# Attention scores as three 64-row products interleaved with half transposes, in one periodic order of all engines

## Chip, cores, metric

The kernel runs on 1 core of one Trainium2 chip. The metric is the device time of one execution in microseconds (us). The program is one launch; the changed part is its first stage.

## The reference

```
q_rot, k_rot = rotate(q), rotate(k)                      # rotary embedding, B=4, H=8, S=576, D=64
scores = q_rot @ k_rot.T / 8;  scores -= max
attn = exp(scores);  attn /= sum + 1e-9;  x = attn @ v   # to (2304, 512)
h = x @ w_in;  g = where(h > 0, h, exp(min(h, 0)) - 1);  x = g @ w_out     # 512 -> 2048 -> 512
out = ((x @ w1) * (x @ w2)) @ w3 @ w_out2                # 512 -> 1024 -> 1024 -> 512
```

All inputs are float32; the weights are drawn so that their words are unpacked from 64-bit words on the chip.

## The kernel before

**Stage one, attention, is the part that the change rewrites.** A unit is one batch and one pair of heads; there are 16 units. The two heads of a pair lie on 64 partitions each (D = 64). For every unit the kernel loads q and k (`load`, L267, on SP's queue), rotates them on POOL (`rope`: two multiplications with the cosine and sine table L284, one addition L287), copies the high part to a reduced-precision form on ACT (`copy_hi`, L94) and makes the low part on POOL (L293). A score is hi*hi + hi*lo + lo*hi. So that one product of 128 rows does two of these terms, `stack` (L363) copies the parts by 12 DMAs of 144 KB a unit into a tile `st` in which high and low lie on top of each other.

**Groups.** A unit has nine score groups (c, j): four blocks c of 128 queries for each of the two heads j, and one group c = 4 for the last 64 queries of both heads at once (`scores`: L388 takes 4 products from `st`; c = 4 takes 6 products of L380, from the block-diagonal tile `diag`, which POOL fills by two small copies, L98). Each group then has a maximum on DVE (L400), an exponential on ACT with the row sums (L404), four 128x128 transposes on TensorE (`turn`, L436, with L444 and L448 for the keys beyond 512) and an evacuation from PSUM, on ACT or DVE in turn (L418, L420). `weigh` multiplies by v (L505, one head in each column half of the array; L495, L499). `norm`, `spread` (POOL, L98) and `norm_turn` (L477, L479) make the reciprocal sums, spread and transpose them; `weighed` (L511) multiplies them in.

**Order.** The order of every engine is written out by hand: a loop over groups n issues group n+2's scores and softmax and group n's transposes, and a table `todo` holds what else comes at each n (rotation, loads, sums, weights). Unit 0 runs its scores from 64-row products (L380), since its stacks would come too late; dummy products (`warm_up`, L610) stand between. 16 weight chunks are fetched and unpacked during the stage (`paced`, L136 on ACT; L139, L142, L145 on DVE).

**The rest** (two feed-forward networks, from L739 on) is untouched but for one call. Its first product C at L739 follows the last product of stage one on TensorE.

```
for kc in range(4):                                             # turn
    pe.transpose(pt[:, kc], pr[:, at_:at_ + P], idt)
...
for z in (1, 2):                                                # scores, L388
    pe.matmul(s[:, n, :288], st[:, j, 0, c * P:c * P + P], st[:, j, z, n * 288:(n + 1) * 288], start=(z == 1), stop=(z == 2))
```

Of the kernel before, what the change touches and what calls it, by code (L numbers as in the profile page):

```python
# [7 lines left out]
F32 = mybir.dt.float32  # L8
F32R = mybir.dt.float32r
# [10 lines left out]
NKC = 5  # L20
SK = S + 64
# [28 lines left out]
SUM_STEP = 3  # L50
MAKE_AT = (133, 64, 104)
# [20 lines left out]
def kernel(  # L72
# [161 lines left out]
    with ExitStack() as c1:  # L234
# [17 lines left out]
        ps_t = c1.enter_context(tc.tile_pool(name="ps_t", bufs=3, space=PSUM, reuse_waits="tile"))  # L252

        tab = tab_p.tile([P, 2, 2, SK], F32, name="tab")
        diag = [cst.tile([P, 2, P], F32R, name=f"diag{i}") for i in range(2)]
        two = cst.tile([P, D], F32, name="two")
        pl1 = cst.tile([P, 384], F32, name="plT1")
        zero = cst.tile([P, 1, 1], F32, name="zero")
        sums_b = [cst.tile([P, 6, 2], F32, name=f"sums{i}") for i in range(3)]
        rb = [cst.tile([P, 2, 2, D], F32, name="rb"), cst.tile([P, 3, 2, D], F32, name="rb2")]  # L260

        raws, hls, stacks, vs = {}, {}, {}, {}

        def load(u, w):
            n = (S, SK)[w]
            raws[u, w] = qk_p.tile([P, 2, n], F32, tag="raw_qk", name="raw_qk", padded_shape=[P, 2, SK])
            nc.sync.dma_start(raws[u, w], (q, k)[w][u[0], u[1]])  # L267

        def load_v(u):
            vs[u] = v_p.tile([P, 2 * NKC * D + P], F32, tag="v", name="v_")  # L270
            nc.sync.dma_start(vs[u], v[u[0], u[1]])

        COLS = (slice(0, S), slice(S, S + SK))
        TAB = (slice(SK - S, SK), slice(0, SK))

        def rope(u, w):

            if u not in hls:
                hls[u] = hl_st[units.index(u) % 2].tile([P, 2, 2 * SK], F32R, tag="hl", name="hl")
            hl, r = hls[u], raws[u, w]  # L280
            hi, lo = hl[:, 0, COLS[w]], hl[:, 1, COLS[w]]

            def turn(z):
                pool.tensor_tensor(r[:, z], r[:, z], tab[:, w, z, TAB[w]], op=ALU.mult)  # L284

            def add():
                pool.tensor_tensor(r[:, 0], r[:, 0], r[:, 1], op=ALU.add)  # L287

            def high():
                copy_hi(hi, r[:, 0], act)  # L290

            def low():
                pool.tensor_tensor(lo, r[:, 0], hi.bitcast(F32), op=ALU.subtract)  # L293
                stack(u, w)

                m = units.index(u) + 2 - w
                if m < len(units):
                    load(units[m], 1 - w)

            return [lambda: turn(0), lambda: turn(1), add, high, low]  # L300

        def first_load(u):

            for w in (0, 1):
                raws[u, w] = qk_p.tile([P, 2, (S, SK)[w]], F32, tag="raw_qk", name="raw_qk", padded_shape=[P, 2, SK])
            for dst, src, at_, to in (
                (tab[:, 1], tables, 0, 352), (raws[u, 1], k[u[0], u[1]], 0, 352), (raws[u, 0], q[u[0], u[1]], 0, 256),
                (tab[:, 1], tables, 352, SK), (raws[u, 1], k[u[0], u[1]], 352, SK), (raws[u, 0], q[u[0], u[1]], 256, S),
            ):
                nc.sync.dma_start(dst[:, :, at_:to], src[:, :, at_:to])  # L310

        def part(u, w, at_, to, eng, hi_eng, lo_eng):

            s, c, t = (SCALE, 1.0)[w], COLS[w].start, TAB[w].start

            def turn(z):
                r = raws[u, w]
                eng.tensor_tensor(r[:, z, at_:to], r[:, z, at_:to], tab[:, 1, z, t + at_:t + to], op=ALU.mult)

            def add():  # L320
                r = raws[u, w]
                eng.tensor_tensor(r[:, 0, at_:to], r[:, 0, at_:to], r[:, 1, at_:to], op=ALU.add)

            def high():
                if u not in hls:
                    hls[u] = hl_st[units.index(u) % 2].tile([P, 2, 2 * SK], F32R, tag="hl", name="hl")
                copy_hi(hls[u][:, 0, c + at_:c + to], raws[u, w][:, 0, at_:to], hi_eng, s)

            def low():
                r, hl = raws[u, w][:, 0, at_:to], hls[u][:, :, c + at_:c + to]  # L330
                if s == 1.0:
                    lo_eng.tensor_tensor(hl[:, 1], r, hl[:, 0].bitcast(F32), op=ALU.subtract)
                else:
                    lo_eng.scalar_tensor_tensor(hl[:, 1], r, s, hl[:, 0].bitcast(F32), op0=ALU.mult, op1=ALU.subtract)

            return [lambda: turn(0), lambda: turn(1), add, high, low]

        def first_rope(u):
            for w, at_, to, eng, steps in (
                (1, 0, 352, dve, (0, 1, 2)), (0, 0, 256, dve, (0, 1, 2)),  # L340
                (1, 0, 352, dve, (3, 4)), (0, 0, 256, dve, (3, 4)), (1, 352, SK, dve, (0, 1, 2, 3, 4)),
            ):
                pieces = part(u, w, at_, to, eng, act, eng)
                for k_ in steps:
                    pieces[k_]()
# [20 lines left out]
        HALF = ((0, 256), (256, 320))  # L366
        sums_t, S_t, pr_t, pt_t = {}, {}, {}, {}

        def scores(g):
            u, c, j = g  # L370
            s = S_t[g] = ps_s.tile([P, 2, 512], F32, tag="s", name="s")
            if c == 4 or u == units[0]:

                d, h = diag[units.index(u) % 2], slice(64 * j, 64 * j + 64) if c < 4 else slice(0, P)
                at_ = S + 64 * (c == 4 or j == 0)
                for n in range(2):
                    if n and g == seq[0]:
                        warm_up(FILL_IN)
                    for i, (a, e) in enumerate(PAIRS):
                        pe.matmul(  # L380
                            s[:, n, :288], hls[u][h, a, c * P:c * P + P] if c < 4 else d[:, a],
                            hls[u][h, e, at_ + n * 288:at_ + (n + 1) * 288], start=(i == 0), stop=(i == 2),
                        )
                return
            st = stacks[u]
            for z in (1, 2):
                for n in range(2):
                    pe.matmul(  # L388
                        s[:, n, :288], st[:, j, 0, c * P:c * P + P], st[:, j, z, n * 288:(n + 1) * 288],
                        start=(z == 1), stop=(z == 2),  # L390
                    )
# [1020 lines left out]
```

## Time and profile before

| what | value |
|---|---|
| device time, median of 3 runs | 1001.48 us (997.84 to 1002.62) |
| profiled execution, first to last instruction (span) | 998.8 us |
| stage one (to the first product of L739) | 298.89 us of the span |
| TensorE (PE) busy | 981.7 us, 98% of the span |
| DVE, ACT, POOL busy | 783.3, 643.0, 234.9 us |
| DMA, mean | 161 GB/s |

The profiled execution is known by its span alone; what lies around the span is not in the profile. Busy time of PE counts a product to its modelled end, and products overlap, so a busy share of 98% does not say that PE could not take more. PE is matmuls, PEld its weight loads, SP the engine that issues the loads.

### The profile page before, as it was taken

How to read it: one execution, taken by the hardware profiler on the slowest of the kernel's cores; microseconds unless marked ns; L12 is line 12 of the kernel's file. 1: busy time of each engine (PE TensorE's matmuls, PEld its weight loads, DVE VectorE, ACT ScalarE, POOL GpSimd, SP SyncE). 2: the span in 40 equal slices, each digit the busy share in tenths (PEclk: the TensorE clock that was granted, in tenths of full speed). 3: DMA queues.
4: the chain of work that ended last, by engine and by line, in shares of the span. 5: the costliest groups of instructions: out<-in, count | busy, mean ns of one | idle time of the engine just before them, and what ended most of it. 6: DMA issues, size and time to landing. Idle time of an engine off the chain costs nothing.

```text
span 998.8 us, 16766 instructions
## 1 busy us (share of the span) xinstructions
PE 981.7 (98%) x5900; PEld 863.3 (86%) x5900; DVE 783.3 (78%) x1467; ACT 643.0 (64%) x1373; POOL 234.9 (24%) x242
## 2 busy tenths in 40 slices
PE   9899999999999999999999999999999999999998
PEld 8677777777769999999999999998899999999997
DVE  6588888888869999998889999665657676675544
ACT  3577776776769687897778877774444454444332
POOL 3688889899660000000000000000000000000000
PEclk9899999999999999999999999999999999999999
DMA  5878787887731446676564686514132243224211
GB/s 186 233 234 243 233 251 231 228 255 208 220 120 44 149 152 204 196 213 205 190 194 145 210 280 208 182 61 148 32 121 84 89 140 85 74 74 149 87 30 63
DMA packets 76930, 160.99 MB, mean 161 GB/s; under 512 B 9520, under 2 KB 18352, under 8 KB 76848
## 3 DMA queue, kind: packets, MB, share of 16 engines
q1 hardware_dynamic: 76848, 159.95, 52.7%
q8 instruction: 46, 0.75, 0.3%
q14 instruction: 36, 0.29, 0.1%
HBM read 107.68 MB, written 25.69 MB: 134 GB/s over the span
## 4 chain that ended last, share of the span: by engine, by line
PE 87%; POOL 4%; DMA 4%; DVE 2%; ACT 1%; issue 1%; SPq 0%; ACTq 0%; DVEq 0%; POOLq 0%
PE y L782 13%; PE A L1213 10%; PE A L739 10%; PE o L1239 9%; PE B L739 7%; PE B L1213 7%; PE yb L783 7%; PE o L505 5%; PE w L1143 4%; PE s L388 4%; PE ptp L436 4%; PE s L380 1%; DVE nm L400 1%; DMA st<-hl 1%; PE warm L610 1%
## 5 line engine op out<-in xcount | busy, mean ns | idle before, releaser
L782 PE MATMUL y<-g,wo 128*128 128x512 f32 x576 | 204.1, 392 | 0.0
L783 PE MATMUL yb<-g,wo 128*128 128x256 f32 x576 | 161.2, 280 | 0.0
L404 ACT ACTIVATE pr<-s,nm 128x576 f32<-128x576 f32 x144 | 106.3, 738 | 50.5 <-DVE nm L400 49.9
L153 DVE TENSOR_TENSOR set<-set 128x512 fp32r<-128x512 f32 (+1 forms) x160 | 98.2, 619 | 41.6 <-ACT set L150 41.2
L782 PEld LDWEIGHTS y<-g,wo 128*128 128x128 f32 x576 | 107.8, 187 | 20.5
L400 DVE TENSOR_REDUCE nm<-s 128x1 f32<-128x576 f32 x144 | 108.0, 751 | 17.9 <-PE s L388 9.7
L1213 PE MATMUL A<-xc,set 128*128 128x384 f32 x576 | 116.1, 336 | 0.2
L1239 PE MATMUL o<-W,g 128*128 128x512 f32 x432 | 111.1, 393 | 0.0
L739 PE MATMUL A<-xf,set 128*128 128x384 f32 x552 | 111.1, 336 | 0.0
L1213 PEld LDWEIGHTS A<-xc,set 128*128 128x128 f32 x576 | 102.4, 188 | 7.8 <-DVE p L1300 1.0
L783 PEld LDWEIGHTS yb<-g,wo 128*128 128x128 f32 x576 | 108.7, 189 | 0.0
L388 PE MATMUL s<-st 128*128 128x288 f32 x480 | 94.0, 318 | 4.5 <-DMA st<-hl 3.6
L739 PEld LDWEIGHTS A<-xf,set 128*128 128x128 f32 x552 | 93.7, 188 | 2.9
L94 ACT ACTIVATE g<-p 128x384 fp32r<-128x384 f32 x48 | 25.2, 526 | 107.8 <-DVE p L1300 71.5
L436 PE MATMUL ptp<-idt,pr 128*128 128x128 f32 x576 | 90.8, 280 | 0.6 <-ACT pr L404 0.6
L1239 PEld LDWEIGHTS o<-W,g 128*128 128x128 f32 x432 | 80.0, 188 | 12.7
L150 ACT ACTIVATE set<-set 128x512 fp32r<-128x512 f32 (+1 forms) x160 | 89.1, 568 | 2.6 <-DMA set<-kept 2.4
L436 PEld LDWEIGHTS ptp<-idt,pr 128*128 128x128 f32 x576 | 65.5, 143 | 29.1 <-DVE ri L460 8.0
L1213 PE MATMUL B<-xc,set 128*128 128x384 f32 x432 | 86.5, 334 | 0.0
L284 POOL TENSOR_TENSOR raw_qk<-raw_qk,tab 128x640 f32<-128x640 f32 (+1 forms) x56 | 85.2, 1521 | 2.2
L739 PE MATMUL B<-xf,set 128*128 128x384 f32 x420 | 84.3, 336 | 0.0
L1213 PEld LDWEIGHTS B<-xc,set 128*128 128x128 f32 x432 | 76.0, 188 | 0.0
(378 smaller groups left out, 1834.0 us busy)
## 6 DMA issues: line engine op xcount, KB each, us to landing
set<-kept SPq DMA_DIRECT2D x120, 256.0 KB, 2.8
st<-hl SPq DMA_DIRECT2D x180, 144.0 KB, 2.6
raw<-w_ SPq DMA_DIRECT2D x32, 512.0 KB, 4.2
kept<-wr SPq DMA_DIRECT2D x40, 256.0 KB, 3.2
raw_qk<-k_ SPq DMA_DIRECT2D x15, 640.0 KB, 5.4
raw_qk<-q_ SPq DMA_DIRECT2D x15, 576.0 KB, 4.4
raw<-w_in_ SPq DMA_DIRECT2D x16, 512.0 KB, 5.2
raw<-w_out_ SPq DMA_DIRECT2D x16, 512.0 KB, 5.3
```

The lines of the kernel that those rows point to most:

```text
L150: act.activation(t[:, 0, :w], t[:, 1, :w].bitcast(F32), ACTF.Copy)
L153: eng.tensor_tensor(t[:, 1, :w], t[:, 1, :w].bitcast(F32), t[:, 0, :w].bitcast(F32), op=ALU.subtract)
L284: pool.tensor_tensor(r[:, z], r[:, z], tab[:, w, z, TAB[w]], op=ALU.mult)
L388: pe.matmul(s[:, n, :288], st[:, j, 0, c * P:c * P + P], st[:, j, z, n * 288:(n + 1) * 288], start=(z == 1), stop=(z == 2),)
L400: dve.tensor_reduce(nm, s[:, :, :288], axis=AX.XY, op=ALU.max, negate=True)
L404: act.activation(pr_t[u, c][:, j].rearrange("p (n i) -> p n i", n=2), s[:, :, :288], ACTF.Exp, bias=nm, accum_out=sums_t[u, hf][:, at_, :1],)
L436: pe.transpose(pt[:, kc], pr[:, at_:at_ + P], idt)
L739: pe.matmul(banks[b][:, :HF], set_w(n, k, a, c), x[:, e, c], start=(start and i == 0), stop=i == 5, skip_group_check=True,)
L782: pe.matmul(y_t[p, o], w_, g[:, c, :512], start=s, stop=t, skip_group_check=True)
L783: pe.matmul(yb_t[p, o // 2][:, o % 2], w_, g[:, c, 512:], start=s and o % 2 == 0, stop=t, skip_group_check=True,)
L1213: pe.matmul(ps[:, :HB], w[:, a, c * P:(c + 1) * P], x[:, c, b], start=(start and i == 0), stop=i == 5, skip_group_check=True,)
L1239: pe.matmul(outs[p, o], g[:, a, o % 3 * P:o % 3 * P + P], wW[f][:, c], start=(f == 0 and i == 0), stop=(f == NG - 1 and i == 2),)
```

## The change

Units, groups, maximum, exponential and the work that follows stage one stay as they are. What is different:

- **Scores** are three products of 64 rows each (hi*hi, hi*lo, lo*hi; `PAIRS`), for each of two column blocks of 288: six products a group (L342). `st` and its 12 DMAs are gone.
- **Transposes** take 64 rows at a time: 64 queries of the exponentials, 128 keys, out 128x64 (`turns` L390, `side_turns` L410, `last_turns` L420). One head's scores use one half of the rows of the array; the half transposes between them use the other half. They are issued alternately.
- **Diagonal** tiles of c = 4 are filled by two DMAs on SP (L298), not by POOL.
- **Rotation**: the two multiplications of a tile are one operation of 128x1152 (`turned` L278); k has 576 columns, not 640. Unit 0 is rotated by DVE, all others by POOL.
- **Sums**: the spread reciprocals of POOL (`spread` L93, tiles rb0 and rb1; `spread4` L454) are transposed among the half transposes.
- **v products** come in five visits a unit (`weigh` L466, 64x128 or 64x64, eight products each; L474 for the keys beyond 512).
- **Unpacking** of weights works in PSUM in between (L499 to L505).
- **Order**: a table of times in one period, `TIMES`, is laid out for all units at a distance `PERIOD`, sorted, and issued in that order. The times set the order of instructions alone; nothing waits for a clock.

The diff, cut to its core:

```diff
+PERIOD = 13.879
+HALF_T = 0.07
+TIMES = {
+    "L1": -38.79, "f": -38.18, "Km1": -35.79, "L0": -22.65, "Km0": -18.40, "Ka0": -15.44, "Ka1": -14.04,
...
+}
+FIRST_LOADS = ((1, "L1"), (1, "L0"), (2, "L1"))
...
-        ps_t = c1.enter_context(tc.tile_pool(name="ps_t", bufs=3, space=PSUM, reuse_waits="tile"))
+        ps_t = c1.enter_context(tc.tile_pool(name="ps_t", bufs=1, space=PSUM, reuse_waits="tile"))
...
+        def turned(u, w):
+            pool.tensor_tensor(raws[u, w], raws[u, w], tab[:, w], op=ALU.mult)
+
+        def added(u, w):
+            pool.tensor_tensor(raws[u, w][:, 0], raws[u, w][:, 0], raws[u, w][:, 1], op=ALU.add)
...
+        def hi_of(u, w):
+            copy_hi(hl_of(u)[:, w, 0], raws[u, w][:, 0], act)
...
+        def diagonal(u):
+            for j in range(2):
+                h = ROWS[j]
+                nc.sync.dma_start(diag[u % 2][h, :, h].bitcast(F32), hls[u][h, 0, :, 512:S].bitcast(F32))
...
-                    for e in range(2):
-                        part = hls[u][64 * j:64 * j + 64, (e, 1 - e)[z == 2]].bitcast(F32)
-                        nc.sync.dma_start(st[64 * e:64 * e + 64, j, z].bitcast(F32), part[:, c:c + S])
...
+                (a, e), h, hl = PAIRS[i], ROWS[j], hls[u]
+                pe.matmul(
+                    S_t[u, c, j][:, n, :288], hl[h, 0, a, c * P:c * P + P], hl[h, 1, e, n * 288:(n + 1) * 288],
+                    start=(i == 0), stop=(i == 2),
+                )
...
+                pe.transpose(
+                    z_t["XY"[l]][:, n:n + 64], pr_t[u, c][ROWS[l], j, kc * P + 64 * j:kc * P + 64 * j + P], idt[ROWS[l], ROWS[l]]
+                )
...
+            for kc in range(4):
+                for j in range(2):
+                    pe.matmul(
+                        o[ROWS[j], n:to], vj[:, j, kc], pT4[:, j, kc] if c == 4 else pT[c // 2][:, j, kc, n:to],
+                        start=(kc == 0 and first), stop=(kc == 3), skip_group_check=True,
+                    )
...
+                elif code[0] == "K" and 0 < u < NU:
+                    w = int(code[2])
+                    event(t, {"m": turned, "a": added, "h": hi_of, "l": lo_of}[code[1]], u, w, first=1.75)
+                elif code == "D" and 0 < u < NU:
+                    event(t, diagonal, u, first=1.75)
...
+            event(1.65, parts[3][4])
+            event(1.70, load, 1, 0)
+            event(1.71, diagonal, 0)
+            event(1.72, load, 2, 1)
...
+            events.sort(key=lambda e: e[:3])
+            for *_, f, args in events:
+                f(*args)
```

**Order on TensorE, in the middle of stage one.** Names: `s` scores, `ptp` and `ptl` transposes, `o` the product with v, `x`, `y`, `z` half transposes. Before:

```order
L505 MATMUL o_3398<-ptT_3258,v__3168 64x256 x4
L436 MATMUL ptp_3405<-idt_58,pr_3348 128x128 x4
L388 MATMUL s_3411<-st_3194 128x288 x4
L436 MATMUL ptp_3433<-idt_58,pr_3348 128x128 x4
L444 MATMUL ptl__3438<-idt_58,pr_3294 128x128
L444 MATMUL ptl__3438<-idt_58,pr_3348 128x128
L388 MATMUL s_3443<-st_3194 128x288 x4
L495 MATMUL o_3398<-plT_3259,v__3168 128x256
L505 MATMUL o_3398<-ptT_3258,v__3168 64x256 x4
L436 MATMUL ptp_3460<-idt_58,pr_3394 128x128 x4
L448 MATMUL ptl__3465<-idt_58,pr_3394 64x128
L388 MATMUL s_3470<-st_3194 128x288 x4
```

With the change:

```order
L410 MATMUL z_2454<-idt_58,pr_2318 128x64
L342 MATMUL s_2439<-hl_1899 128x288
L410 MATMUL z_2454<-idt_58,rb0_126 128x64
L466 MATMUL o_2461<-pT0_121,v__2018 64x128 x8
L355 MATMUL s_2479<-idt_58,pr4_2221 128x64 x2
L356 MATMUL s_2479<-r4_113,mask_111 128x64
L361 MATMUL s_2479<-hl_1899,diag1_110 128x288 x6
L342 MATMUL s_2493<-hl_2198 128x288
L390 MATMUL y_2495<-idt_58,pr_2404 128x64 x2
```

Runs of four scores and four transposes have become one score, one or two half transposes, one score and so on (the last two rows go on alternating). A v visit (L466) follows two groups, the first one here together with the sums of c = 4 (L355, L356) and its six scores (L361). The transposes of `rb0` (POOL's spread sums, L410) stand just ahead of that visit.

**Order on POOL and on SP, middle of stage one.** Names: `hl` high and low parts, `raw_qk` loaded q and k, `rb`, `rb0`, `rb1`, `r4` spread sums, `st` stacks. POOL before, from the end of q's rotation of one unit to the low part of k of the next:

```order
L287 TENSOR_TENSOR raw_qk_897<-raw_qk_897 128x576
L293 TENSOR_TENSOR hl_1049<-raw_qk_897,hl_1049 128x576
L98 TENSOR_SCALAR rb_117<-ri_1254 128x256
L284 TENSOR_TENSOR raw_qk_1024<-raw_qk_1024,tab_108 128x640
L98 TENSOR_SCALAR diag1_110<-hl_1049 64x2x64 x2
L284 TENSOR_TENSOR raw_qk_1024<-raw_qk_1024,tab_108 128x640
L287 TENSOR_TENSOR raw_qk_1024<-raw_qk_1024 128x640
L293 TENSOR_TENSOR hl_1278<-raw_qk_1024,hl_1278 128x640
```

POOL with the change, from the low part of q of unit 2 on:

```order
L293 TENSOR_TENSOR hl_420<-raw_qk_278,hl_420 128x576
L93 TENSOR_SCALAR rb1_127<-recip0_118 128x256
L293 TENSOR_TENSOR hl_420<-raw_qk_233,hl_420 128x576
L278 TENSOR_TENSOR raw_qk_472<-raw_qk_472,tab_108 128x1152
L93 TENSOR_SCALAR rb0_126<-recip1_119 128x256
L278 TENSOR_TENSOR raw_qk_520<-raw_qk_520,tab_108 128x1152
L454 TENSOR_SCALAR r4_113<-two_112,recip0_118 128x64
L281 TENSOR_TENSOR raw_qk_520<-raw_qk_520 128x576
L281 TENSOR_TENSOR raw_qk_256<-raw_qk_256 128x576
L293 TENSOR_TENSOR hl_705<-raw_qk_520,hl_705 128x576
```

In the change `rb0` of unit 1 stands behind the multiplication (L278) of k of unit 4, and the low part of q of unit 3 behind both. SP with the change, from the diagonal of that unit 2 on (`raw_qk_472` is k of unit 4, `raw_qk_520` q of unit 3):

```order
L298 DMA diag0_109<-hl_420 64x2x64 x2
L271 DMA raw_qk_472<-k_ 128x1152
L103 DMA raw_490<-w_in_ 128x512
L271 DMA raw_qk_520<-q_ 128x1152
L275 DMA v__525<-v_ 128x768
L298 DMA diag1_110<-hl_705 64x2x64 x2
```

The load of k stands right behind the two diagonal DMAs, which wait for POOL's low part of q (L293) of the unit; before, k's load stood behind four stack DMAs instead and POOL filled the diagonal itself.

**Order on ACT and SP at the start.** `pr` is the exponential, `z` a weight chunk in PSUM. ACT before:

```order
L94 ACTIVATE hl_181<-raw_qk_127 128x352
L94 ACTIVATE hl_181<-raw_qk_126 128x256
L94 ACTIVATE hl_181<-raw_qk_127 128x288
L404 ACTIVATE pr_207,sums0_114<-s_193,nm_205 128x576
L404 ACTIVATE pr_207,sums0_114<-s_209,nm_216 128x576
L404 ACTIVATE pr_233,sums0_114<-s_224,nm_231 128x576
L94 ACTIVATE hl_181<-raw_qk_126 128x320
L418 ACTIVATE ptT_246<-ptp_248 128x4x128
L404 ACTIVATE pr_233,sums0_114<-s_257,nm_264 128x576
L94 ACTIVATE hl_268<-raw_qk_134 128x640
```

ACT with the change, from the table's scaling on:

```order
L640 ACTIVATE tab_108<-tab_108 128x1152
L499 ACTIVATE z_215<-raw_209 128x512
L89 ACTIVATE hl_240<-raw_qk_229 128x576
L379 ACTIVATE pr_244,sums0_115<-s_218,nm_226 128x576
L89 ACTIVATE hl_240<-raw_qk_146 128x576
L379 ACTIVATE pr_244,sums0_115<-s_246,nm_264 128x576
```

SP with the change, from the third weight chunk on:

```order
L103 DMA raw_213<-w_out_ 128x512
L271 DMA raw_qk_229<-q_ 128x1152
L298 DMA diag0_109<-hl_188 64x2x64 x2
L271 DMA raw_qk_233<-k_ 128x1152
L298 DMA diag1_110<-hl_240 64x2x64 x2
L271 DMA raw_qk_256<-k_ 128x1152
```

The high part of q of unit 1 (from `raw_qk_229`, L89) now stands ahead of the first exponential (L379); before, the first four exponentials stood ahead of unit 1's first high part. On SP, q of unit 1, the diagonal of unit 0 and k of unit 2 (`raw_qk_233`) follow three weight chunks.

## Rows read from the trace of the kernel before

**Rows 1.** The page: span, and busy time of each engine.
```profile
span 998.8 us, 16766 instructions
...
PE 981.7 (98%) x5900; PEld 863.3 (86%) x5900; DVE 783.3 (78%) x1467; ACT 643.0 (64%) x1373; POOL 234.9 (24%) x242
```

**Rows 2.** Stretches: length, busy us (x) of PE, PEld, DVE, ACT, POOL; PEclk, DMA, GB/s.
```profile
0.00:10.00 10.00, 8.96 (x57) 8.96 (x58) 4.55 (x12) 2.20 (x3) 1.51 (x12) 1.00 0.76 245
30.00:40.00 10.00, 6.85 (x32) 5.03 (x30) 3.30 (x7) 3.72 (x8) 6.38 (x7) 0.68 1.02 288
160.00:280.00 120.00, 117.45 (x888) 89.73 (x888) 102.03 (x178) 87.22 (x202) 101.37 (x102) 1.00 0.83 233
```

**Rows 3.** Timeline of PE, places of one unit: start, us, operation, idle before it.
```profile
51.44 1.06 PE L380 MATMUL s<-hl,diag 128*128 128x288 f32 x6
...
288.45 1.03 PE L380 MATMUL s<-hl,diag 128*128 128x288 f32 x6
...
298.89 1.31 PE L739 MATMUL C<-xf,set 128*128 128x384 f32 x6
```

**Rows 4.** Timeline of PE: 64-row products, then one mode after another.
```profile
12.15 1.07 PE L380 MATMUL s<-hl 64*128 64x288 f32 x9
...
14.53 1.05 PE L380 MATMUL s<-hl 64*128 64x288 f32 x6 [0.21 <-ACT pr L404]
...
152.35 0.69 PE L380 MATMUL s<-hl,diag 128*128 128x288 f32 x4
...
152.48 0.56 PE L380 MATMUL s<-hl,diag 128*128 128x288 f32 x3
...
152.97 1.08 PE L505 MATMUL o<-ptT,v__1780 128*64 128x256 f32 x8
153.99 0.66 PE L436 MATMUL ptp<-idt,pr 128*128 128x128 f32 x4
...
297.55 0.34 PE L499 MATMUL o<-plT,v__3617 128*64 128x64 f32 x4
297.71 1.25 PE L505 MATMUL o<-ptT,v__3617 128*64 128x320 f32 x8
```

**Rows 5.** POOL by form, 40 to 280 us: line, shapes, count, busy us, mean ns, idle.
```profile
L284 POOL TENSOR_TENSOR raw_qk<-raw_qk,tab 128x640 f32<-128x640 f32 x26 | 40.8, 1568 | 1.1
L284 POOL TENSOR_TENSOR raw_qk<-raw_qk,tab 128x576 f32<-128x576 f32 x27 | 39.9, 1477 | 1.2
...
L287 POOL TENSOR_TENSOR raw_qk<-raw_qk 128x576 f32<-128x576 f32 x14 | 20.9, 1495 | 1.0
L293 POOL TENSOR_TENSOR hl<-raw_qk,hl 128x576 fp32r<-128x576 f32 x14 | 20.0, 1430 | 12.0 <-ACT hl L94 11.9
L98 POOL TENSOR_SCALAR rb<-ri 128x256 f32<-128x256 f32 x28 | 13.8, 494 | 1.1 <-DVE ri L460 1.0
```

**Rows 6.** DMA issues of L267 on SP: ns min/median/max; below, us to landing.
```profile
L267 SPq DMA_DIRECT2D raw_qk<-k_ x15: 328/587/606, 4.7 to 235.4; - x15
L267 SPq DMA_DIRECT2D raw_qk<-q_ x15: 545/602/1245, 11.3 to 247.8; - x15
...
DMA to landing us min/median/max: 4.1/4.5/7.3
```

**Rows 7.** Timeline, all engines: first exponential; PE's wait for the first stacks.
```profile
13.64 0.74 ACT L404 ACTIVATE pr<-s,nm 128x576 f32<-128x576 f32 x1 [2.82 <-DVE nm L400]
...
34.36 1.30 PE L388 MATMUL s<-st 128*128 128x288 f32 x4 [3.15 <-DMA st<-hl]
```

**Rows 8.** DVE and ACT by form, 40 to 280 us.
```profile
L400 DVE TENSOR_REDUCE nm<-s 128x1 f32<-128x576 f32 x127 | 95.3, 751 | 9.1 <-PE s L388 5.2 <-PE s L380 1.9 <-PE ptp L436 0.3
...
L142 DVE SCALAR_TENSOR_TENSOR pair<-raw,pair 128x512 int32<-128x512 int32 x16 | 17.6, 1102 | 0.0
...
L404 ACT ACTIVATE pr<-s,nm 128x576 f32<-128x576 f32 x127 | 93.8, 738 | 36.3 <-DVE nm L400 35.6
...
L94 ACT ACTIVATE hl<-raw_qk 128x576 fp32r<-128x576 f32 x14 | 9.6, 685 | 17.1 <-POOL raw_qk L287 17.1
```

More of the change, by code (lines that the diff above doesn't have):

```diff
@@ new lines @@
+        recip = [cst.tile([P, 9], F32, name=f"recip{i}") for i in range(3)]
+        pT = [cst.tile([P, 2, 4, 256], F32, name=f"pT{i}") for i in range(2)]
+        pT4 = cst.tile([P, 2, 4, D], F32, name="pT4")
+        side = [cst.tile([P, 512], F32, name=f"side{i}") for i in range(2)]
+        rb = [cst.tile([P, 256], F32, name=f"rb{i}") for i in range(2)]
+        side4 = cst.tile([P, 192], F32, name="side4")
+        units = [(b, hp) for b in range(B) for hp in range(4)]
+        NU = len(units)
@@ L269, in load_v @@
         def load_v(u):
[L270 to L276, printed above, removed]
-            if u not in hls:
[L279 to L345, printed above, removed]
+            vs[u] = v_p.tile([P, 12 * D], F32, tag="v", name="v_")
+            nc.sync.dma_start(vs[u], v[units[u][0], units[u][1]])
@@ L366 @@
[L366 to L391, printed above, removed]
@@ L509, in weighed @@
-        def weighed(u, hf):
-            r = R_t.pop((u, hf))
-            dve.tensor_tensor(r, o_t.pop((u, hf)), r, op=ALU.mult)
-        def paced(n, key, src):
-            steps = []
-            def step(i):
-                if i == 0:
-                    steps.extend(weight_steps(key))
-                steps[i]()
-            at(max(0, n - DLEAD), fetch_w, key, src)
-            for i, d in enumerate(STEPS):
-                at(n + d, step, i, first=i == 0)
-        units = [(b, hp) for b in range(B) for hp in range(4)]
@@ new lines, in slot_of, with scores, one_of @@
+        def slot_of(u, c, j):
+            S_t[u, c, j] = ps_s.tile([P, 2, 512], F32, tag="s", name="s")
+            return S_t[u, c, j]
+        def scores(u, c, j):
+            def one_of(n, i):
+                if n == 0 and i == 0:
+                    slot_of(u, c, j)
+                (a, e), h, hl = PAIRS[i], ROWS[j], hls[u]
[3 more added lines that the diff above has]
+                )
+            return [lambda n=n, i=i: one_of(n, i) for n in range(2) for i in range(3)]
@@ new lines, in side4_out, with norm, spread @@
+        def side4_out(u, eng):
+            evacuate(side4, S_t[u + 1, 4, 0][:, 1, 288:480], eng)
+        def norm(u, at_, to):
+            dve.tensor_reduce(recip[u % 3][:, at_:to], sums[u % 3][:, at_:to], axis=AX.X, op=ALU.add)
+            dve.reciprocal(recip[u % 3][:, at_:to], recip[u % 3][:, at_:to])
+        def spread(u, hf):
+            r = recip[u % 3][:, 4 * hf:4 * hf + 4].rearrange("p (c e) -> p c e", e=1).to_broadcast([P, 4, D])
+            copy_hi(rb[hf].rearrange("p (c d) -> p c d", d=D), r, pool)
@@ L616 @@
             pool.memset(zero, 0.0)
-            for sums in sums_b:
-                pool.memset(sums[:, :, 1:], 1e-9)
-            first_load(units[0])
-            load(units[1], 1)
+            for s_ in sums:
+                pool.memset(s_[:, :, 1:], 1e-9)
+            first_load()
+            load(1, 1)
             nc.sync.dma_start(idt, ident)
-            load_v(units[0])
-            load(units[1], 0)
+            load_v(0)
             dve.memset(warm, 0.0)
```

490 lines of the change are left out of this document (256 added, 234 removed), and 11 rows, old and new, of the table TIMES.

## Prediction

> **What bounds the kernel now.** I read the page first: PE is busy 98% of a span of 998.8 us [rows 1], and nothing behind stage one is touched, so the question is where stage one ends. The timeline of PE gives that: the first product of L739 starts at 298.89. The six products of c = 4, once a unit, start at 51.44 in unit 1 and at 288.45 in unit 15 [rows 3]: (288.45 - 51.44) / 14 = 16.93 us a unit, and 10.44 from the last to L739. The table of stretches shows in 160 to 280 us PE busy 117.45 of 120, POOL 101.37, DVE 102.03, ACT 87.22, at a granted clock of 1.00 (2.4 GHz) [rows 2]. So PE sets the pace, and POOL has 14.3 us of work in each 16.93 (101.37 / 120 x 16.93), little less than PE. The start has one hole: PE waits 3.15 us for the first stacks at 34.36 [rows 7], in a stretch of mean clock 0.68 [rows 2], which is part at 1.2 GHz.
>
> **PE's work with the change.** Products of 288 columns follow each other by 152.48 - 152.35 = 0.13 us; take 0.14 with entries [rows 4]. Nine 64-row products, three on one row half and six on the other, took 1.07 us, and six took 1.05 [rows 4]: the halves do run beside each other. So 48 scores a unit take 48 x 0.14 = 6.7, the 88 half transposes lie beside them, and I add 0.3 for those that outlast: 7.0. A visit of L505 takes 153.99 - 152.97 = 1.02 with one change of tiling in it [rows 4]. From the last score (152.35 + 3 x 0.13 = 152.74) to it are 0.23, so 0.10 more than a step; six 64-row scores in 1.05 less 6 x 0.13 leave up to 0.27 at the other end. I take 0.17 for each change, near the middle. The visit itself is then 0.85; four such visits of eight 128-column products have the same columns: 3.4. Two of them end with a pair of 256-column side products (L474), half the work of a visit, 0.43 each: 0.86. The visit of 64 columns and the three small sums: L499's four records took 297.71 - 297.55 = 0.16 [rows 4], so about 0.05 a step, 10 and 8 steps: 0.5 and 0.45. c = 4: 6 x 0.13 = 0.8. Five visits are entered and left, and c = 4 follows one: 11 changes x 0.17 = 1.9. Sum 7.0 + 3.4 + 0.86 + 0.5 + 0.45 + 0.8 + 1.9 = **14.9 us a unit**, 2 less than now. Bounds 14.2 (changes at 0.10) to 16.0 (at 0.27).
>
> **The loop over POOL and SP.** The order shows a ring. After POOL's low part of q of one unit, SP issues two diagonal DMAs, then the load of k two units on. POOL's next long operation needs that k, and the low part of q of the next unit stands behind it. Between, POOL has only a spread and one low part. The pieces:
> - two issues on SP, 0.59 to 0.60 each [rows 6]: 1.2;
> - landing of k: 4.1 at least, 4.5 in the middle, 7.3 at worst [rows 6]; the 12 stack DMAs are gone, so near the least: 4.2, and 0.1 to start;
> - the 1152-element multiplication, twice (k, then q): no such row. Two of 576 give 2 x 1.477 = 2.95; the 91 ns between 1.477 and 1.568 for 64 elements more [rows 5] scale to 2.3 (1.477 + 9 x 0.091). I take 2.65, between: 5.3;
> - a spread, 0.494 [rows 5], 0.45 with DVE somewhat less busy, and r4, half of it or a bit more: 0.28;
> - two additions of 576 at 1.495 and a low part at 1.430 [rows 5], which idle DVE shortens a little: 2.86 + 1.42.
>
> Sum 1.2 + 4.3 + 5.3 + 0.73 + 2.86 + 1.42 = **15.8 us a unit**, bounds 15.0 (2.3 a multiplication, landing 4.1) to 16.9 (2.95, landing 4.5, the rows' means for the rest). It is longer than PE's 14.9, and PE waits for it: rb0, which PE transposes, is made behind the long operation. ACT's high part, 0.685 [rows 8], lies beside the second addition. DVE (14.4 us of 16.93 now) and ACT (12.3) [rows 2] get no more work: nine maxima of 0.751 and nine exponentials of 0.738 a unit stay [rows 8], and the columns to evacuate are the same. I cost them at nothing; if PSUM's single x, y and z tiles make PE wait for them, that is the rival of a longer ring. The stacks' 12 DMAs were covered by POOL's and PE's work except for the 3.15 us at 34.36 [rows 7].
>
> **The start gets worse.** ACT has the first exponential behind unit 1's high part of q. That needs POOL's multiplication of k of unit 2, whose load stands on SP behind unit 0's diagonal, and that behind DVE's low part of q, which stands behind two unpacking steps of the first weight chunk. By rows: tables, q, k, v and three chunks are 3.9 MB ahead at 245 GB/s [rows 2], so the chunk is there at about 15.5. ACT's step 0.7, DVE's two steps about 1.1 each [rows 8], a maximum 0.75 and the low part 0.5: 19.7. Two issues 1.2, landing 4.2: 25.1. Two multiplications 5.3 and one addition 1.43: 31.9. High part 0.685: first exponential at **32.6**, where it was 13.64 [rows 7]. PE has two PSUM tiles for scores and stands idle some 20 us; it will fall to 1.2 GHz there. Then the ring runs once more before the first rb0: second addition and low part (34.7), DMAs and landing (40.2), multiplication (42.9), spread: 43.4. By the table's order c = 4 of unit 0 stands behind two groups and a visit after those transposes, 2.9 of PE's 14.9: 46.3; PE comes out of its idle time behind its order, so I add 1: 47.3.
>
> **The sum.** Units 0 to 12 go by the ring, the last three, with no k left to load, by PE: 47.3 + 12 x 15.8 + 3 x 14.9 = 281.6 for c = 4 of unit 15. From there three and a half visits, the last group and its half transposes, some 8.5 us of PE work with waits between: 10, as now. L739 at 291.6, against 298.89: **7.3 us less**. Span 998.8 - 7.3 = 991.5; the median of the runs is 1001.5, 2.7 above this span, so I say 994.2. The start loses 10 to 12 us, the periods win 14 x 1.1 to 1.3 and the last three more.
>
> **Rivals.**
> - *PE cannot be fed so fast* (slower). Scores and half transposes are 136 loads and products in 7.0 us, 0.051 each. The rows show 0.04 in a burst of four [rows 4], and nothing as dense over microseconds; a v visit goes at 0.13. Above 0.058 PE's period passes the ring's 15.8 (7.9 + 136 x 0.058); above 0.066 it passes 16.93. At 0.070 it is 17.4, and the end 47.3 + 15 x 17.4 + 10 = 318.3: 19 slower, 1021. The Trainium skill, "TensorE: Matmul & The Clock Gate", section "Wait — 56ns, not 53.3ns?", states two floors: about 25 ns start to start, and about 62 ns per product where hardware decode is off. The burst of 0.04 a record speaks against the second; by the second the period would be 7.9 + 136 x 0.062 = 16.3 and the time 1005, an estimate from that page. Chance 0.24.
> - *Row halves do not overlap when scores and transposes mix* (slower): 48 x 0.13 + 88 x 0.05 = 10.6 in place of 7.0 is 18.5 a unit, 47.3 + 15 x 18.5 + 10 = 334.8, 36 slower: 1037. The nine in 1.07 speak against it. Chance 0.05.
> - *The ring is longer* (landing of 4.5 and more, 2.95 a multiplication, ACT late with the high part, or PE's single x, y, z tiles waiting for their evacuations): 16.4 to 17.0 gives 0 to 7 more than now, 1001 to 1009. Chance 0.17.
> - *The ring is shorter than PE's work*: 14.9 a unit, 47.3 + 15 x 14.9 + 10 = 280.8, 18 less: 983; with the start's chain shorter by 5, 978. Chance 0.12.
> - My forecast, a ring of 15.4 to 16.3: 989 to 1000. Chance 0.42, of which some 0.29 are below 996.5.
>
> **How the numbers follow.** A measurement of this kernel tells a change from none at about 0.5%, 5 us. Faster: 0.29 + 0.12 = 0.41. Same: 0.13 of the forecast, 0.06 of the longer ring, 0.04 of the first rival: 0.23. Slower: the rest, 0.36. The range of 8 in 10 goes from 980 (most of the shorter ring) to 1020 (the first rival up to 0.069); the likeliest case alone is 989 to 1000.
>
> **What would show it.** Right: c = 4 of successive units 15.8 apart in the middle; POOL's waits there for a DMA of k, one a unit, and PE's for POOL's rb0; the first exponential at 32 to 33, PE idle before it; no PE wait for stacks. Wrong: PE without idle time at 16.4 or more a unit (feeding, or changes of tiling dearer than 0.27); half transposes that start only at a score's end (no overlap); PE's waits named by DVE or ACT evacuations; a first exponential before 25.

## The result, and the profile after

The change makes the kernel **slower: 1015.23 us in the median (1011.14 to 1017.72) against 1001.92 (997.84 to 1002.62), a ratio of 1.0145 with a 95% interval of 1.0114 to 1.0177.** That is a small loss, but clear of the noise, since the interval leaves out 1. (The 1001.92 is the median of four runs; the prediction had three of them, 1001.48.) The prediction said 994.2 and gave "slower" 0.36. The profiled execution has a span of 1013.2, 14.4 more than before.

The page of the changed kernel, span and busy times, answers to [rows 1]:

```profile
span 1013.2 us, 20015 instructions
...
PE 964.7 (95%) x7692; PEld 870.4 (86%) x7692; DVE 758.6 (75%) x1463; ACT 652.1 (64%) x1406; POOL 200.1 (20%) x168
```

PE is less busy, in a longer span: it waits. Where, the timeline of PE tells (change; start, us, operation; c = 4 is L361 now, the next stage L737), answering to [rows 3]:

```profile
47.87 1.71 PE L361 MATMUL s<-hl,diag 128*128 128x288 f32 x6
...
64.74 1.03 PE L361 MATMUL s<-hl,diag 128*128 128x288 f32 x6
...
247.31 1.05 PE L361 MATMUL s<-hl,diag 128*128 128x288 f32 x6
...
262.50 1.03 PE L361 MATMUL s<-hl,diag 128*128 128x288 f32 x6
...
277.69 1.04 PE L361 MATMUL s<-hl,diag 128*128 128x288 f32 x6
...
299.44 1.03 PE L361 MATMUL s<-hl,diag 128*128 128x288 f32 x6
...
311.19 1.33 PE L737 MATMUL C<-xf,set 128*128 128x384 f32 x6
```

These are units 0, 1, 12, 13, 14 and 15. Four things are to be seen. Unit 1 comes 64.74 - 51.44 = 13.3 us later than before. From unit 0 to 12 a unit takes (247.31 - 47.87) / 12 = 16.6. Units 13 and 14 take 15.2. Unit 15 takes 21.75. From unit 1 to unit 15 the change needs 234.7 where the kernel before needed 237.0: with so uneven units it wins 2.3 us, and it has lost 13.3 by then. Then 11.75 to L737 in place of 10.44, and 702.0 from there to the end in place of 699.9. 13.3 - 2.3 + 1.3 + 2.1 = 14.4. Of the last 2.1, product by product on PE, 1.1 are lost in the first 10 us of the next stage; the rest comes in one place some 300 us later, where e1_ring, which has the same products there, loses nothing.

PE's own share in the middle is in the change's table of stretches, 60 to 240 us, busy 168.09 of 180 (the first number behind the length). In the table of waits, 60 to 280 us, it waits most for POOL's spread sums:

```profile
60.00:240.00 180.00, 168.09 (x2589) 141.96 (x2590) 137.71 (x269) 138.27 (x327) 134.35 (x107) 0.99 0.38 130
```

```profile
PE z L410 <- POOL rb L93: 9.6, 11, 2.3
```

What POOL waits for is in the change's table of waits of POOL, 60 to 250 us (waited for, us in total, times, longest):

```profile
POOL raw_qk L278 <- DMA raw_qk<-k_: 37.2, 12, 3.9
POOL hl L293 <- ACT hl L89: 7.7, 10, 1.2
POOL raw_qk L278 <- DMA raw_qk<-q_: 5.2, 6, 1.4
```

The wait for k is there once a unit, as the order had shown. The timelines of POOL and SP (change) over one turn of the ring:

```profile
182.04 1.40 POOL L293 TENSOR_TENSOR hl<-raw_qk,hl 128x576 fp32r<-128x576 f32 x1
183.42 0.40 POOL L93 TENSOR_SCALAR rb<-recip 128x256 f32<-128x256 f32 x1
184.41 1.41 POOL L293 TENSOR_TENSOR hl<-raw_qk,hl 128x576 fp32r<-128x576 f32 x1 [0.59 <-ACT hl L89]
188.98 2.65 POOL L278 TENSOR_TENSOR raw_qk<-raw_qk,tab 128x1152 f32<-128x1152 f32 x1 [3.16 <-DMA raw_qk<-k_]
191.57 0.42 POOL L93 TENSOR_SCALAR rb<-recip 128x256 f32<-128x256 f32 x1
191.94 2.67 POOL L278 TENSOR_TENSOR raw_qk<-raw_qk,tab 128x1152 f32<-128x1152 f32 x1
194.56 0.35 POOL L454 TENSOR_SCALAR r<-two,recip 128x64 f32<-128x64 f32 x1
```

```profile
183.47 1.30 SPq L298 DMA_DIRECT2D diag<-hl  x2
184.83 0.59 SPq L271 DMA_DIRECT2D raw_qk<-k_  x1
185.52 0.38 SPq L103 DMA_DIRECT2D raw<-w_out_  x1
185.99 0.39 SPq L271 DMA_DIRECT2D raw_qk<-q_  x1
```

POOL ends q's low part at 183.44, SP issues the two diagonal DMAs until 184.77 and then the load of k, POOL can go on at 188.98. The new 1152-element operation is 2.65.

At the start, in the change's timelines of ACT and PE:

```profile
31.42 0.68 ACT L89 ACTIVATE hl<-raw_qk 128x576 fp32r<-128x576 f32 x1 [15.23 <-POOL raw_qk L281]
32.01 0.72 ACT L379 ACTIVATE pr<-s,nm 128x576 f32<-128x576 f32 x1
```

```profile
32.88 3.16 PE L342 MATMUL s<-hl 64*128 64x288 f32 x12 [20.70 <-ACT pr L379]
```

The first exponential starts at 32.01, where it was 13.64 [rows 7], behind unit 1's high part of q, and PE has been idle for 20.70. Then PE waits once more, until 43.06, for rb0 of unit 0, which POOL ends at 43.01.

### The profile page after: what moved, and what is told of

Same layout as the page of the kernel before. It is cut to its first block, busy times and chain, and to the rows that moved or that the text cites. A ratio compares the mean times of both kernels' runs of the same rounds, so it can differ in the third digit from the quotient of the medians.

```text
span 1013.2 us, 20015 instructions
## 1 busy us (share of the span) xinstructions
PE 964.7 (95%) x7692; PEld 870.4 (86%) x7692; DVE 758.6 (75%) x1463; ACT 652.1 (64%) x1406; POOL 200.1 (20%) x168
## 4 chain that ended last, share of the span: by engine, by line
PE 75%; POOL 8%; DMA 8%; DVE 3%; ACT 2%; issue 2%; SPq 1%; POOLq 0%; DVEq 0%; ACTq 0%
PE y L780 13%; PE A L1211 10%; PE A L737 9%; PE o L1237 9%; PE B L1211 7%; PE B L737 7%; PE yb L781 7%; PE w L1141 4%; DMA raw_qk<-q_ 4%; POOL raw_qk L278 4%; DMA raw_qk<-k_ 3%; PE o L466 3%; PE s L342 2%; POOL raw_qk L281 1%; POOL hl L293 1%
## 5 line engine op out<-in xcount | busy, mean ns | idle before, releaser
L342 PE MATMUL s<-hl 64*128 64x288 f32 x768 | 134.6, 323 | 24.6 <-ACT pr L379 24.3
L342 PEld LDWEIGHTS s<-hl 64*128 64x128 f32 x768 | 109.5, 194 | 43.6 <-ACT pr L379 31.7
L379 ACT ACTIVATE pr<-s,nm 128x576 f32<-128x576 f32 x144 | 106.7, 741 | 25.8 <-DVE nm L369 23.9
L737 PE MATMUL A<-xf,set 128*128 128x384 f32 x552 | 111.2, 336 | 1.0 <-DVE p L797 0.9
L737 PEld LDWEIGHTS A<-xf,set 128*128 128x128 f32 x552 | 93.7, 188 | 4.3 <-DVE p L797 1.3
L89 ACT ACTIVATE g<-p 128x384 fp32r<-128x384 f32 x48 | 25.2, 526 | 107.8 <-DVE p L1298 71.5
L278 POOL TENSOR_TENSOR raw_qk<-raw_qk,tab 128x1152 f32<-128x1152 f32 x30 | 79.3, 2646 | 66.7 <-DMA raw_qk<-k_ 52.4
L737 PE MATMUL B<-xf,set 128*128 128x384 f32 x420 | 84.3, 336 | 0.0
L737 PEld LDWEIGHTS B<-xf,set 128*128 128x128 f32 x420 | 72.6, 188 | 1.0
```

The costliest lines, as they stand in the source:

```text
L278: pool.tensor_tensor(raws[u, w], raws[u, w], tab[:, w], op=ALU.mult)
L342: pe.matmul(S_t[u, c, j][:, n, :288], hl[h, 0, a, c * P:c * P + P], hl[h, 1, e, n * 288:(n + 1) * 288], start=(i == 0), stop=(i == 2),)
L379: act.activation(p_.rearrange("p (n i) -> p n i", n=2), S_t[u, c, j][:, :, :288], ACTF.Exp, bias=S_t.pop((u, c, j, "m")), accum_out=sums[u ...
L737: pe.matmul(banks[b][:, :HF], set_w(n, k, a, c), x[:, e, c], start=(start and i == 0), stop=i == 5, skip_group_check=True,)
```

## Experiments

Theory A: the loss is three things in the order of the work: a start that is a chain of loads, POOL and spread sums; the ring over POOL and SP; and early work for the next stage that falls into the last unit. Theory B: TensorE itself, fed with more and smaller products and changing its tiling more often, cannot take less than about 16.4 us a unit, the mean of units 0 to 14.

**e1_ring: cut the ring.**

```diff
-    "L1": -38.79, ... "L0": -22.65,
+    "L1": -51.6, ... "L0": -30.0,
-        qk_p = pool0("qk", 3)
+        qk_p = pool0("qk", 5)
```

> Five buffers for loaded q and k in place of three, and the loads of k a period earlier, those of q before the diagonal DMAs, so that no load on SP waits for POOL's low part of q any more. Nothing else is changed. Theory A (the ring over POOL and SP set the 16.4 us of a unit): c = 4 comes every 15.2 us through the middle, as it did in units 13 and 14 where no load was left, POOL's waits for DMAs of k and q (42 us) are gone; 12 x 1.2 = 14 us less, and some 4 us at the start, where the load of k of unit 3 no longer stands behind the diagonal of unit 1: about 995 us, 0.993 to 1.000 of before. Theory B (TensorE cannot be fed faster, or its changes of tiling set 16.4): the spacing stays at 16.2 to 16.5 and only the start gives: 1009 to 1013, 1.01 of before.

Measured: 994.73 us, 0.9944 of before (0.9925 to 0.9963). The timeline of PE in e1_ring, units 4, 5, 14, 15 and the next stage:

```profile
105.24 1.04 PE L361 MATMUL s<-hl,diag 128*128 128x288 f32 x6
...
120.42 1.04 PE L361 MATMUL s<-hl,diag 128*128 128x288 f32 x6
...
257.22 1.04 PE L361 MATMUL s<-hl,diag 128*128 128x288 f32 x6
...
279.14 1.79 PE L361 MATMUL s<-hl,diag 128*128 128x288 f32 x6
...
292.32 1.31 PE L737 MATMUL C<-xf,set 128*128 128x384 f32 x6
```

Every unit but the last takes 15.2, (257.22 - 105.24) / 10, and PE has no idle time left, as the table of stretches of e1_ring says (busy 180.00 of 180 us, in the change 168.09):

```profile
60.00:240.00 180.00, 180.00 (x2856) 153.87 (x2856) 150.82 (x297) 149.22 (x356) 143.59 (x113) 1.00 0.39 134
```

Theory B has fallen for the middle: the same products in the same order on PE take 15.2. How they stand there, the timeline of PE in e1_ring shows (some products of one score group):

```profile
124.07 0.29 PE L342 MATMUL s<-hl 64*128 64x288 f32 x1
124.08 0.35 PE L390 MATMUL x<-idt,pr 64*128 64x64 f32 x3
124.21 0.29 PE L342 MATMUL s<-hl 64*128 64x288 f32 x1
124.26 0.29 PE L390 MATMUL x<-idt,pr 64*128 64x64 f32 x2
```

Here two scores start 0.14 apart with three half transposes between. Over 60 to 240 us of e1_ring the middle value is 0.13 with two between (200 times) and 0.23 with three (150 times): 0.044 and 0.058 a product.

**e8_kfirst: take the diagonal DMAs out of the ring alone.**

```diff
-    "L1": -38.79,
+    "L1": -39.1,
```

> One number of the changed kernel's table: the load of k stands ahead of the two diagonal DMAs on SP instead of behind them (still behind POOL's low part of q, whose buffer it takes; three buffers). If the ring is a sum of its pieces, this takes out the two issues of 0.6 us each and nothing else: c = 4 every 15.2 to 15.6 us in units without sums on POOL, where the change took 15.8 to 16.6, and 10 to 16 us less in all: about 1002. If the landing of q, which is issued later, is what POOL waits for next, part of it comes back: 1004 to 1010.

Measured: 1002.30 us, 1.0023 of before (1.0008 to 1.0038), 12.9 less than the change (12 by the ratios). Units 0 to 13 took (248.72 - 46.23) / 13 = 15.6, where the change took 16.5. Two issues of 0.6 us, moved behind the load on one queue, were worth 0.9 us a unit: they are a piece of the ring. POOL's waits for q went from 5.2 to 12.5 us, as the second half of the expectation had it, and took part of the gain back.

**e11_qfirst: the weight chunk behind q.**

```diff
-    ... "f": -38.18,
+    ... "f": -36.3,
```

> One number of the changed kernel's table: the weight chunk of each unit is fetched behind the loads of q and v instead of ahead of q; everything else as in the change, three buffers. If what the ring takes over its pieces (16.6 against 15.85 a unit in units 0 to 12) is mostly the late landing of q, POOL's waits for q (0.3 to 1.4 us in eight units) go and the unit comes to 15.85 to 16.2: 5 to 9 us less, 1006 to 1010. If k's landing and ACT's high part make the rest, 2 to 4 us less: 1011 to 1013.

Measured: 1010.74 us, 1.0112 (1.0084 to 1.0140), 4.5 less than the change in the medians (3.3 by the ratios), whose ranges overlap, so that the times alone do not settle it. In the profiled execution units 0 to 12 took (240.60 - 46.81) / 12 = 16.15 in place of 16.6, and POOL's waits for q fell from 5.2 to 0.9 us. So, by the trace, about half of what the ring took over its pieces was the chunk ahead of q (4.3 to 5.7 of 9.8 us).

**e6_same: half transposes on the same rows as the scores beside them.** As e1_ring, with

```diff
-                        z_t["XY"[l]] = ps_t.tile([P, 512], F32, tag="xy"[l], name="xy"[l])
+                        z_t["YX"[l]] = ps_t.tile([P, 512], F32, tag="yx"[l], name="yx"[l])
...
-                        steps(t, turns(u + du, c, int(code[1])), HALF_T)
+                        steps(t, turns(u + du, c, 1 - int(code[1])), HALF_T)
```

and the same exchange in the side and last turns and the evacuations.

> As e1_ring (five buffers), but the half transposes between the scores of one head take the same 64 rows of the array as these scores, not the other 64: the two PSUM tiles and their evacuations change places, every product stays. If the row halves run beside each other in the steady state, this takes it away: 88 half transposes at about 0.05 come on top of the scores, the unit goes from 15.2 to 18 to 20 us and the time to 1035 to 1070. If they were serial already: 15.2 and about 995.

Measured: 1082.45 us, 1.0826 (1.0806 to 1.0846), more than expected. The timeline of PE in e6_same:

```profile
113.59 0.38 PE L342 MATMUL s<-hl 64*128 64x288 f32 x1
113.80 0.28 PE L390 MATMUL y<-idt,pr 64*128 64x64 f32 x2
113.90 0.38 PE L342 MATMUL s<-hl 64*128 64x288 f32 x1
114.12 0.28 PE L390 MATMUL y<-idt,pr 64*128 64x64 f32 x2
114.21 0.37 PE L342 MATMUL s<-hl 64*128 64x288 f32 x1
```

A score with two half transposes takes 0.31 here and 0.13 on separate rows. A unit is 20.86 (112.30 to 133.16) against 15.20: the overlap of row halves, which the kernel before showed once, for nine products [rows 4], is worth 5.7 us a unit.

**e2_hi: the misplaced high part of unit 1.** In the changed kernel, for unit 1 only, its high and low parts (below) and likewise its diagonal and the load of k of unit 3 come later:

```diff
-                    event(t, {"m": turned, ... "l": lo_of}[code[1]], u, w, first=1.75)
+                    event(t, {"m": turned, ... "l": lo_of}[code[1]], u, w, first=5.3 if u == 1 and code[1] in "hl" else 1.75)
```

> Only the order at the start: unit 1's high and low parts of q and k (and the diagonal and the load behind them) come after the first three exponentials. Theory A (the start is set by the chain loads, POOL, the spread sums rb0 of unit 0): the first exponential is at 18 to 19 us in place of 32.0, but c = 4 of unit 0 stays at 46 to 49, since rb0 still stands behind the multiplication of k of unit 3: time within 3 us of the change, 1012 to 1016. Theory B (the one misplaced high part costs the idle time of TensorE): c = 4 of unit 0 at 34 to 38 and 10 us or more less.

Measured: 1014.97 us, 1.0139 (1.0106 to 1.0173), no different from the change. The first exponential came at 18.19, 13.8 earlier, and c = 4 of unit 0 at 48.50. The timeline of POOL in e2_hi has the reason:

```profile
40.66 2.61 POOL L278 TENSOR_TENSOR raw_qk<-raw_qk,tab 128x1152 f32<-128x1152 f32 x1 [5.03 <-DMA raw_qk<-k_]
43.23 0.41 POOL L93 TENSOR_SCALAR rb<-recip 128x256 f32<-128x256 f32 x1
```

rb0 of unit 0 is ready at 43.6 here and at 43.0 in the change, whatever ACT does. The idle time of PE at the start was real and cost nothing by itself.

**e3_x and e4_both: early sums of the next stage later**, in the change and in e1_ring:

```diff
-X_AT = (15.06, 15.25, 15.45, 15.65)
-PAIR_AT = (15.35, 15.85)
+X_AT = (15.06, 15.25, 15.70, 16.0)
+PAIR_AT = (15.80, 16.1)
```

> Only the order at the end of stage one: two of the four early sums of the next stage's input, and both early weight pairs, come after the spread sums of unit 15. Theory A (this work on POOL and ACT stretched the last unit from 15.2 to 21.8 us): last unit 16 to 18 us, 4 to 6 us less, 1008 to 1011. Theory B (the last unit is long for its own sake, the last groups having nothing to lie beside): 21 to 22 us as in the change, same time or longer by what the early work now lacks.

> e1_ring and e3_x together. If both causes hold and are separate: the sum of both gains, about 18 + 5: 990 us, 0.985 to 0.995 of before. If the last unit's length came from the ring's delay, no better than e1_ring.

Measured: e3_x 1013.76 us, 1.0138 (1.0098 to 1.0178), inside the change's spread; the last unit fell to 18.5 (279.94 to 298.42), but L737 then came 16.7 behind c = 4 in place of 11.75. e4_both 991.58 us, 0.9920 (0.9893 to 0.9947), with a last unit of 19.5. So the work does stretch the last unit; moving it gives 3 us back in the medians of e4_both against e1_ring, whose intervals overlap, or nothing, since the next stage needs it.

**e7_nox: all of that work behind stage one.** As e1_ring, with X_AT from 17.4 on and PAIR_AT at 17.42 and 17.6.

> As e1_ring, but all four early sums of the next stage's input and both early weight pairs are issued at the end of stage one, behind everything else. Theory A (they stretch the last unit): c = 4 of unit 15 comes 15.2 to 16 us after that of unit 14, where e1_ring took 21.9; the first product of the next stage then waits for them, 20 us or more after that c = 4 instead of 13.2, so that the time is the same or up to 8 us longer than e1_ring. Theory B (the last unit has nothing to lie beside): still 21 to 22.

Measured: 1005.08 us, 1.0052 (1.0034 to 1.0071). The timeline of PE in e7_nox, units 14, 15 and the next stage:

```profile
256.97 1.04 PE L361 MATMUL s<-hl,diag 128*128 128x288 f32 x6
...
272.15 1.04 PE L361 MATMUL s<-hl,diag 128*128 128x288 f32 x6
...
284.90 0.44 PE L737 MATMUL C<-xf,set 128*128 128x384 f32 x1 [0.91 <-ACT set L151]
```

The last unit takes 15.18 like all others, so nothing else stretched it. I had expected L737 late; it came 7 us earlier than in e1_ring, and the stage then starved, as the first 20 us of it in the table of stretches of e7_nox show, PE busy 9.13 at a granted clock of 0.52; the whole is 10 us longer than e1_ring:

```profile
284.90:304.90 20.00, 9.13 (x23) 6.62 (x24) 5.54 (x8) 7.26 (x12) 12.75 (x8) 0.52 0.00 0
```

**e5_start: the start in another order.** As e4_both, with q of unit 1 loaded ahead of the weight chunks, the first chunk unpacked later, unit 1's high and low parts behind the first exponentials, and

```diff
-    ... "Km1": -35.79,
+    ... "Km1": -18.5,
```

> As e4_both (five buffers, early work later), with the start reordered: q of unit 1 is loaded ahead of the weight chunks, the first chunk is unpacked behind three exponentials, unit 1's high and low parts come behind four or five exponentials, and POOL multiplies k one unit later, behind the spread sums rb0 of the unit before. Theory (the start is the chain load, POOL, spread sums): first exponential at 15 to 17 us, c = 4 of unit 0 at 27 to 32 instead of 44.4, the unit still 15.2: 12 to 17 us less than e4_both, 975 to 980, 0.975 to 0.981 of before. If POOL falls behind at the start, some of it is lost in units 1 and 2.

Measured: 1004.13 us, 1.0038 (1.0023 to 1.0053). The start did as expected, the first exponential at 14.88 and c = 4 of unit 0 at 30.63. The middle did not: 16.8 a unit, some of them 17 to 18.2. The timelines of POOL and PE in e5_start:

```profile
94.77 0.40 POOL L93 TENSOR_SCALAR rb<-recip 128x256 f32<-128x256 f32 x1 [4.72 <-DVE recip L447]
95.14 5.22 POOL L278 TENSOR_TENSOR raw_qk<-raw_qk,tab 128x1152 f32<-128x1152 f32 x2
```

```profile
100.72 0.43 PE L356 MATMUL s<-r,mask 128*128 128x64 f32 x2 [1.42 <-POOL r L454]
```

Both multiplications now stand between the spread sums and r4, for which PE's L356 waits, and POOL's spread sums wait for PE's next unit: a ring of my own making, worth 1.6 us a unit. The next run puts the multiplication back and has 15.2.

**e9_best and e10_split.** e9_best has the start of e5_start with Km1 at its old place from unit 4 on; in both, ACT's high part of an early sum comes 0.16 period behind the sum and the sums are late:

```diff
+    ... {(2, "m1"): 9.0, (3, "m1"): 17.6}.get((u, code[1:]), 1.75))
...
+            event((n + 0.16) * PERIOD, early_high, k_)
```

> Five buffers and early loads (e1_ring), the start of e5_start, but POOL's multiplication of k is back at its old place from unit 4 on, ahead of the spread sums; for the last unit the early sums of the next stage are issued later, and ACT's high part of each comes 0.16 period behind the sum, so that ACT does not stand behind POOL. Theory: c = 4 of unit 0 at 30 to 32, then every 15.2 us (e5_start took 16.8 to 18.2, because both multiplications stood ahead of r4, which the sums of c = 4 need), last unit 17 to 20: e4_both less 12 to 15: 974 to 981, 0.974 to 0.982 of before. If the 16.8 of e5_start had another cause (the start's order carried along), it stays at 16 or more and the time above 995.

> e1_ring with the same late and split early work of the next stage as in e9_best, the start as in the change. If ACT standing behind POOL's sums made the last unit long, it takes 16 to 18 us (21.9 in e1_ring, 19.5 in e4_both) and the time is 2 to 5 us under e1_ring; if only POOL's place was at fault, as e4_both: 991 to 992.

Measured: **e9_best 978.92 us, 0.9793 of before (0.9758 to 0.9828)**, faster than both kernels. e10_split 991.19 us, 0.9921 (0.9892 to 0.9949), 3.5 under e1_ring in medians whose ranges overlap, with a last unit of 17.2, where e4_both had 19.5: where ACT stands was part of that unit's length (the sums stand at slightly other times too). The time is that of e4_both all the same (991.58), since L737 comes 13.9 behind c = 4, there 12.3. The timeline of PE in e9_best, units 0, 1, 2, 14, 15, next stage:

```profile
30.61 1.06 PE L361 MATMUL s<-hl,diag 128*128 128x288 f32 x6
...
46.57 1.04 PE L361 MATMUL s<-hl,diag 128*128 128x288 f32 x6
...
61.77 1.03 PE L361 MATMUL s<-hl,diag 128*128 128x288 f32 x6
...
244.09 1.05 PE L361 MATMUL s<-hl,diag 128*128 128x288 f32 x6
...
261.34 1.03 PE L361 MATMUL s<-hl,diag 128*128 128x288 f32 x6
...
275.27 1.31 PE L741 MATMUL C<-xf,set 128*128 128x384 f32 x6
```

Of its 12.3 us against e10_split the start gives 14.3 (c = 4 of unit 0 at 30.61, there at 44.89), and unit 1, at 16.0 in place of 15.1, takes 0.9 back; the stages behind take another 1.3.

## Why the prediction was wrong

The order of things was right, the sum was not: L737 was put at 291.6 and came at 311.2. Two steps failed, the ring's sum and the last unit. Either alone would have left the change slower by 4 to 6 us; only with both right would it have been faster. That 1015 lies in the stated range of 980 to 1020 is luck: the room at its upper end was made for a PE that cannot be fed, which did not happen.

- **Start: right.** First exponential 32.6, measured 32.01; c = 4 of unit 0 47.3, measured 47.87, by the chain that was named. (3.9 MB at 245 GB/s are 15.9 and not 15.5; ACT's step on the chunk began at 15.57.) Two small errors offset: rb0 was ready at 43.0 in place of 43.4, and from there to c = 4 it took 4.9 in place of 3.9. That ACT's misplaced high part was not the cost, but the ring's first turn, is in the same chain; e2_hi shows it.
- **PE's work: right in size.** 14.9 a unit was said, 15.2 is what PE takes without waits (e1_ring): 0.6 over two units. Its terms were off both ways: from start to start in units 4 to 13 of e1_ring, scores and half transposes take 7.8 a unit, not 7.0, and all the rest 7.4, not 7.9, with each change of tiling counted to the product before it.
- **The ring: the mechanism was right, its size too small.** Of the pieces nothing is far off: one multiplication 2.65 (2.65), spread 0.42 (0.45), r4 0.35 (0.28), issues 1.30 (1.2), landing 188.98 - 184.83 = 4.15 (4.2 and 0.1). They sum to 15.75, what the turn shown took from one multiplication of k to the next, and single units took about 15.85. The mean was 16.6, 9.8 us more over twelve units than 12 x 15.8. The failed step is the one that listed POOL's waits in the ring: q was costed at its multiplication alone, though the order showed a 512 KB weight chunk between k and q on SP. The change's timelines of POOL and SP separate the rest. From the multiplication of k at 40.01 to that at 240.24 twelve turns take 200.2, 10.5 more than 12 times the sum's 15.81. The waits for q add 4.8. ACT's late high part of q, in two turns, adds 2.8. SP, with 1.42 a turn from POOL's low part to the load of k in place of 1.2, adds 2.6. Landings of k, 4.31 in the mean and 0.15 to start in place of 4.2 and 0.1, add 1.9. Sums of weights on POOL, in two turns, which the list left out, add 1.4. POOL's listed operations took 3.0 less than costed. The longer ring, as a rival, had 16.4 to 17.0 and a chance of 0.17. Its period is what happened, by ACT's high part and longer landings as it said, but more by the wait for q, which it did not name; its time of 1001 to 1009 lacked the last unit.
- **The last unit: missed.** "The last three, with no k left to load, by PE" was true of two. The change lays the next stage's early sums into unit 15, where POOL does eight operations of 1.3 to 1.85 us for them around the spread sums, and ACT waits for POOL; the sum had no term for it. 6.9 us there and 1.8 in the tail. e7_nox shows the first, and that it cannot simply be left away. What made the tail 1.8 longer stays open.
- **"PE cannot be fed so fast": wrong, for this program.** It had 0.24 of the chance. The rate that was doubted, 0.051 a product, was nearly held through the units of e1_ring: 7.8 us for the 136 of a unit is 0.058, changes of tiling among them. So of the two floors that the Trainium skill states in "TensorE: Matmul & The Clock Gate", section "Wait — 56ns, not 53.3ns?", the one of about 62 ns per product, given for hardware decode off, did not bind here: e1_ring starts scores 0.13 apart with two half transposes between, 0.044 a product.
- **Row halves serial: wrong**, and dearer than I had put it: 20.86 a unit (e6_same), not 18.5. On the same rows a half transpose starts 0.21 to 0.22 behind a score (113.59 to 113.80), where a score follows a score by 0.13.
- Changes of tiling, 0.17 each, were never measured alone. They are inside the 15.2 that PE takes.

0.6 + 9.8 + 0.6 + 6.9 + 1.8 = 19.7, which is, but for rounding, the 19.6 that L737 was missed by.

## What to carry to other kernels

Follow each queue once round: if a load waits for an engine's last use, and that engine's next long work waits for that load, the ring's sum is a floor of the period whatever the busy shares say, and two more buffers, with the loads moved up, can be worth more than a rewrite of the products (20 us here, e1_ring against the change). A table of a periodic order has no guard at its ends: check what the first and the last period carry besides, since here both lost more than the middle won (13.3 us at the start, and 6.9 from unit 15 on, against the 5.7 won in units 1 to 14). Idle time of the bounding engine at the start is a symptom; find the last chain that ends there before you pay for removing it (e2_hi).

## What the runs showed of the hardware

- Products on different row halves of TensorE overlap almost wholly when they alternate: 0.13 us for a score and two half transposes (e1_ring), 0.31 on the same rows (e6_same).
- The clock fell to its lower level (1.2 GHz) while PE was idle from 12 to 33 us and was still there in most of 40 to 50 us, although PE was busy 7.5 of these 10. The prediction had added 1 us for PE's late return; from rb0 to c = 4 it took 2.0 more than the 2.9 of PE's work. The change's table of stretches (the granted clock stands third from the end):

```profile
20.00:30.00 10.00, 0.00 (x0) 0.00 (x0) 0.12 (x1) 0.00 (x0) 5.18 (x3) 0.50 0.23 66
40.00:50.00 10.00, 7.53 (x68) 6.46 (x70) 4.38 (x8) 4.82 (x11) 8.41 (x5) 0.53 0.25 101
```

- One POOL operation over 1152 elements takes 2.65 us. Two over 576 took 2.95 in the kernel before [rows 5], but two additions of 576 take 2.80 in the changed kernel (at 179.28), where POOL's operations are shorter throughout: of the 0.3, joining them saves about 0.15.
